# Re-spacing the memory projections, moving the zeroing and the first loads to other engines, and merging the memory update into the attention stage

## The chip, the cores and the metric

The kernel runs on one core of one Trainium2 chip. The metric is device time in microseconds (us), lower is better. Most executions of one kernel agree within a few tenths of a per cent. The engines are called as in the profile: PE is TensorE (matmuls), DVE is VectorE, ACT is ScalarE, POOL is GpSimd, and SP is SyncE, which here only issues DMA transfers. "1.00" as granted clock means that PE ran at full speed.

## The reference

The output is the concatenation of two independent parts over 2048 tokens of width 1024:

```python
def _A_ref(...):                        # complex diagonal state-space scan
    for t in range(L):
        h = Lam_bar[None, :] * h + Bu[:, t, :]
    y = 2.0 * einsum(hseq, Cmat).real + x * Dskip

def _B_ref(x, mem0, Wq, Wk, Wv, Wo, seg_len):     # 64 segments of 32 tokens, 8 memory tokens, 32 heads x 128
    mem = mem0
    for s in range(n_seg):
        h = concatenate([mem, x[segment s]])       # 40 tokens
        q, k, v = h @ Wq, h @ Wk, h @ Wv
        p = softmax(mask(q @ k.T * scale))
        o = (p @ v) @ Wo
        mem = o[:, :M, :]                          # memory for the next segment
        outs.append(o[:, M:, :])
```

The recurrence over `mem` looks serial. The kernel guesses the memory of all segments, computes everything in parallel with the guess, computes the new memory, and sets a flag if it differs too much; only then would it go round again. The trace holds one pass.

## The kernel before

The kernel runs in stages, with times read from the trace of before: part A (0 to 336 us); phase 1a, the K and V projections of part B (PE's last one ends at 834 us); phase 1b (844.5 to 1147 us), the Q projections, the guess of the memory and the projections of that guess ("memory projections"); the attention stage (1147 to 1655 us), 32 units of 4 segments x 16 heads; and the memory update with its flag (to the end).

Phase 1b goes through eight blocks of 512 weight columns. Each memory projection needs three 1 MB weight tiles (Wq, Wk, Wv); the Wq tile can be shared with the Q projection of the same block. The guess is ready only after block 2, so blocks 3 to 5 do two memory projections each, the second one for an early block:

```python
    wp  = tile_pool(name="p2_w", bufs=5)        # weights of Q and memory projections
    sp1 = tile_pool(name="p2_stg1", bufs=1)     # staging of the memory projections' results
    ...
    LAG = 3
    early = list(range(LAG))
    for hb in range(HB):
        wq = q_x(hb)                            # 128 matmuls of 512 columns, stores qT
        ...                                     # three steps of the guess
        if hb >= LAG:
            memproj(hb, wq)                     # stores qmT, kmT, vm of this block
            if early:
                memproj(early.pop(0))
    for hb in early:
        memproj(hb)
```

The attention stage first zeroes its block-diagonal buffers, then loads two units ahead. The rows of V that belong to the memory ("vmx") come in 16 small transfers per unit, half issued by SP and half by ACT. ACT then copies the memory columns of K and Q into place, behind its own issues:

```python
        for t in qmp + vmx + PTx + PTm + PTxm + PTmm:
            Gp.memset(t[:], 0.0)                                   # L458, POOL
        def load(u):
            nc.sync.dma_start(d["qT"][:], ...)
            nc.scalar.dma_start(d["kT"][:], ...)
            nc.sync.dma_start(km_u, ...); nc.sync.dma_start(qm_u, ...)
            nc.scalar.dma_start(d["v"][:], ...)
            for j in range(J):
                for b in range(4):
                    ...
                    (nc.sync if (j * 4 + b) % 2 == 0 else nc.scalar).dma_start(dst, src)   # L482
            S.activation(d["kT"][:, :, :, 0:M], km_u[:], ACT.Copy)   # L484, the K copy
            S.activation(<diagonal of qmp>, qm_u, ACT.Copy)
        ...
        load(0); load(1); front(0)
        for u in range(NU):
            if u + 1 < NU:
                front(u + 1)        # scores (PE), softmax (DVE, POOL, ACT), transposes (DVE)
            back(u)                 # probabilities x V (PE)
            if u + 2 < NU:
                load(u + 2)
            ...                     # half an output projection
```

The order of this text is not the order on PE: the build reorders the instructions of each engine within their dependencies, and fixes that order.

The memory update stands after the attention stage, in pools of its own: for each of 8 blocks 32 matmuls (L401), then DVE's differences and squares, two sums by matmul, and at the end the flag.

## Time and profile before

| | before |
|---|---|
| median of 15 runs | 1691.72 us (1685.87 to 1694.79) |
| span of the profiled run | 1686.6 us |
| PE busy | 1460.4 us, 87% |
| mean granted clock | 0.946 |

The first view is the page of the profile of before, its busy table and two rows of its slices (each digit is the busy share, or the clock, of one fortieth of the span, in tenths):

```profile
PE 1460.4 (87%) x14297; PEld 762.0 (45%) x14297; DVE 819.9 (49%) x1851; ACT 425.5 (25%) x793; POOL 165.4 (10%) x257
...
PE   4888989889999999999799988892888788877776
...
PEclk9899999899999999999999999896899989999998
```

PE is the engine that bounds the kernel, and one slice stands out: the digit 2, around 1160 us, where the attention starts, with a clock digit of 6 to 8 around it.

The windows view shows phase 1b in five stretches. Its columns are: the stretch, its length and PE's busy time, then the busy time of the other engines, and at the end the granted clock, the mean busy share of the DMA engines (as it is counted, it can come out a little above 1), and GB/s.

```profile
844.50:966.00 121.50, 117.22 (x917) 58.17 (x918) 37.14 (x89) 21.74 (x38) 2.10 (x6) 0.98 0.51 159
966.00:1010.00 44.00, 38.29 (x282) 20.57 (x280) 10.98 (x18) 9.90 (x19) 0.00 (x0) 0.92 0.76 226
1010.00:1050.00 40.00, 34.74 (x256) 18.40 (x255) 11.10 (x18) 9.27 (x18) 0.00 (x0) 0.96 0.88 254
1050.00:1090.00 40.00, 33.81 (x237) 17.41 (x235) 9.89 (x17) 8.40 (x17) 0.00 (x0) 0.87 0.83 249
1090.00:1147.00 57.00, 57.00 (x366) 28.81 (x363) 15.82 (x25) 13.70 (x25) 0.00 (x0) 1.00 0.63 185
```

PE is idle for 17.2 us in the three middle stretches, where the doubled memory projections are (44.00 - 38.29, and so on), and not at all in the last. The stretches with idle time also have a lower clock. What PE waits for there is in the view of waits, PE in phase 1b (what waited, on what: us in total, times, longest):

```profile
PE s_p L633 <- DMA p_w<-in_B_Wv_dram: 9.4, 3, 5.0
PE p_p L679 <- DMA p_w<-in_B_Wq_dram: 4.4, 2, 3.5
PE s_p L624 <- ACT s_stvd L253: 2.0, 3, 0.7
PE p_p L679 <- DVE p_stq L255: 1.7, 2, 1.4
```

Weight loads and evacuations, then. The evacuations are late because DVE in turn waits until a store has emptied the single staging buffer (view of waits, DVE, 955 to 1145 us):

```profile
DVE s_st L255 <- DMA b_qmT_s<-s_st: 20.7, 3, 13.1
```

The start of the attention is in the timeline of ACT (start, duration, engine, line; "ACTq" is ACT issuing a transfer, "x4" four of them; in brackets the idle time before, and what ended it). For the same time the windows view gives one line:

```profile
1156.37 7.11 ACTq L482 DMA_DIRECT2D s_vmx<-b_vm_s  x4
1163.59 0.63 ACT L484 ACTIVATE s_kT<-s_km 128x512 bf16<-128x512 bf16 x1 [15.31 <-DMA s_vmx<-b_vm_s]
...
1167.94 5.79 ACTq L482 DMA_DIRECT2D s_vmx<-b_vm_s  x8
1173.77 0.63 ACT L484 ACTIVATE s_kT<-s_km 128x512 bf16<-128x512 bf16 x1 [9.03 <-DMA s_vmx<-b_vm_s]
```
```profile
1147.00:1181.80 34.80, 3.10 (x258) 2.99 (x257) 9.38 (x19) 5.98 (x13) 17.01 (x17) 0.55 0.78 243
```

In both units the K copy comes directly after a batch of vmx issues, and PE, which needs the K copy for its scores, is busy 3.1 of 34.8 us at about half the clock.

### The profile page before, as it was taken

How to read it: one execution, taken by the hardware profiler on the slowest of the kernel's cores; microseconds unless marked ns; L12 is line 12 of the kernel's file. 1: busy time of each engine (PE TensorE's matmuls, PEld its weight loads, DVE VectorE, ACT ScalarE, POOL GpSimd, SP SyncE). 2: the span in 40 equal slices, each digit the busy share in tenths (PEclk: the TensorE clock that was granted, in tenths of full speed). 3: DMA queues.
4: the chain of work that ended last, by engine and by line, in shares of the span. 5: the costliest groups of instructions: out<-in, count | busy, mean ns of one | idle time of the engine just before them, and what ended most of it. 6: DMA issues, size and time to landing. Idle time of an engine off the chain costs nothing.

```text
span 1686.6 us, 33729 instructions
## 1 busy us (share of the span) xinstructions
PE 1460.4 (87%) x14297; PEld 762.0 (45%) x14297; DVE 819.9 (49%) x1851; ACT 425.5 (25%) x793; POOL 165.4 (10%) x257
## 2 busy tenths in 40 slices
PE   4888989889999999999799988892888788877776
PEld 2443434444444444444345444441545444544444
DVE  8999999632121221121123322222656666566664
ACT  7742322111111111111121122221322232322322
POOL 1100000020000000000000000004222222222220
PEclk9899999899999999999999999896899989999998
DMA  2420000395334343441473488866444545444423
GB/s 88 138 82 19 26 19 13 101 318 188 113 110 155 113 159 106 149 152 51 151 234 117 125 243 262 246 186 211 132 153 138 158 137 160 157 143 153 138 93 108
DMA packets 223112, 233.72 MB, mean 139 GB/s; under 512 B 61152, under 2 KB 194016, under 8 KB 222952
## 3 DMA queue, kind: packets, MB, share of 16 engines
q1 hardware_dynamic: 152880, 130.13, 24.8%
q10 hardware_dynamic: 68024, 95.04, 17.2%
q0 software_dynamic: 2048, 6.30, 1.1%
q8 instruction: 114, 1.87, 0.5%
q14 instruction: 46, 0.38, 0.1%
HBM read 150.99 MB, written 80.45 MB: 137 GB/s over the span
## 4 chain that ended last, share of the span: by engine, by line
PE 55%; DVE 27%; DMA 7%; POOL 5%; ACT 3%; issue 2%; SPq 1%; POOLq 0%; ACTq 0%; DVEq 0%
PE p_p L309 13%; PE p_p L322 13%; PE p_p L679 12%; PE s_pY L577 6%; DVE s_PTx L535 4%; DVE a_wr L177 2%; DVE a_wi L178 2%; POOL s_Sxx L502 2%; PE s_pO L555 2%; PE s_pO L554 2%; POOL s_Pxx L509 2%; DVE s_Sxx L498 1%; DVE s_sumx L505 1%; DVE s_mxx L501 1%; ACT s_Sxx L503 1%
## 5 line engine op out<-in xcount | busy, mean ns | idle before, releaser
L577 PE MATMUL s_pY<-b_Wo,s_oT 128*128 128x512 bf16 x1024 | 250.4, 399 | 4.6 <-issue 2.7
L679 PE MATMUL p_p<-g_shared,p_w 128*128 128x512 bf16 x1024 | 230.6, 386 | 17.6 <-POOL s_PTmm L458 10.2
L309 PE MATMUL p_p<-g_shared,p_w 128*128 128x512 bf16 x1024 | 224.3, 381 | 3.4 <-DMA p_w<-in_B_Wk_dram 3.4
L322 PE MATMUL p_p<-p_w,g_shared 128*128 128x512 bf16 x1024 | 224.8, 379 | 0.0
L679 PEld LDWEIGHTS <-p_w 128*128 128x128 bf16 x1024 | 100.9, 99 | 144.5 <-issue 14.8
L577 PEld LDWEIGHTS <-s_oT 128*128 128x128 bf16 x1024 | 99.7, 102 | 127.4 <-issue 24.6
L309 PEld LDWEIGHTS <-p_w 128*128 128x128 bf16 x1024 | 100.0, 98 | 124.0 <-DMA p_w<-in_B_Wk_dram 3.5
L322 PEld LDWEIGHTS <-g_shared 128*128 128x128 bf16 x1024 | 98.4, 98 | 118.4 <-issue 3.0
L554 PE MATMUL s_pO<-s_PTx,s_v 128*128 128x128 bf16 x512 | 77.8, 235 | 81.5 <-DVE s_PTx L535 73.0
L255 DVE CAST p_stk<-p_p 128x512 bf16<-128x512 f32 x64 | 44.3, 692 | 192.2 <-PE p_p L309 185.9
L255 DVE CAST p_st<-p_p 128x512 bf16<-128x512 f32 x64 | 44.3, 692 | 181.5 <-PE p_p L322 181.5
L255 DVE CAST p_stq<-p_p 128x512 bf16<-128x512 f32 x64 | 44.2, 691 | 163.4 <-PE p_p L679 145.6
L535 DVE STREAM_TRANSPOSE s_PTx<-s_Pxx 32x512 bf16<-32x512 bf16 x128 | 89.9, 703 | 45.1 <-POOL s_Pxx L509 43.7
L554 PEld LDWEIGHTS <-s_v 128*128 128x128 bf16 x512 | 52.8, 105 | 89.6 <-issue 45.3
L253 ACT ACTIVATE p_st<-p_p 128x512 bf16<-128x512 f32 x64 | 38.2, 597 | 201.5 <-PE p_p L322 201.5
L253 ACT ACTIVATE p_stk<-p_p 128x512 bf16<-128x512 f32 x64 | 38.2, 597 | 179.6 <-PE p_p L309 168.0
L165 PEld LDWEIGHTS <-g_shared 128*128 128x128 bf16 x512 | 51.7, 102 | 70.3 <-issue 21.8
L253 ACT ACTIVATE p_stq<-p_p 128x512 bf16<-128x512 f32 x64 | 37.7, 597 | 168.9 <-PE p_p L679 134.9
L165 PE MATMUL a_ur<-a_xT,g_shared 128*128 128x512 bf16 x256 | 70.0, 411 | 9.1 <-DVE a_ta L173 9.1
L556 ACT ACTIVATE s_oT<-s_pO 128x512 bf16<-128x512 f32 x128 | 70.0, 593 | 25.6 <-PE s_pO L555 25.0
L458 POOL MEMSET s_qmp<- 128x2048 bf16 x3 | 5.4, 1805 | 721.2 <-DMA b_v_s<-p_st 484.3
L555 PE MATMUL s_pO<-s_PTm,s_vmx 128*128 128x128 bf16 x512 | 74.9, 236 | 0.6
(197 smaller groups left out, 1931.4 us busy)
## 6 DMA issues: line engine op xcount, KB each, us to landing
s_kT<-b_kTa_s ACTq DMA_DIRECT2D x34, 640.0 KB
b_kTa_s<-p_stk ACTq DMA_DIRECT2D x8, 2560.0 KB
p_w<-in_B_Wq_dram SPq DMA_DIRECT2D x19, 1024.0 KB
s_v<-b_v_s ACTq DMA_DIRECT2D x34, 512.0 KB
p_w<-in_B_Wk_dram ACTq DMA_DIRECT2D x16, 1024.0 KB
b_v_s<-p_st SPq DMA_DIRECT2D x8, 2048.0 KB
b_qT_s<-p_stq SPq DMA_DIRECT2D x16, 1024.0 KB
s_qT<-b_qT_s SPq DMA_DIRECT2D x32, 512.0 KB
```

The costliest lines, as they stand in the source:

```text
L165: PE.matmul(u[:], BT[i][:, kc, pc * 128:(pc + 1) * 128], xT[:, kc, :], start=(kc == 0), stop=(kc == KC - 1))
L177: V.tensor_tensor_scan(wr[:], rb, wr[:], 0.0 if ini is None else ini[:, 0:1], ALU.mult, ALU.add)
L253: self.nc.scalar.activation(out, in_, ACT.Copy)
L255: self.nc.vector.tensor_copy(out, in_)
L309: PE.matmul(p[:], w[1][:, c, h4 * 128:(h4 + 1) * 128], xT[:, c, tb * 512:(tb + 1) * 512], start=(c == 0), stop=(c == KC - 1))
L322: PE.matmul(p[:], xT[:, c, tt * 128:(tt + 1) * 128], w[2][:, c, :], start=(c == 0), stop=(c == KC - 1))
L535: V.transpose(ptx[q, j, :, :].rearrange("p h k -> p (h k)"), Px[q, :, :].rearrange("p h k -> p (h k)"))
L554: PE.matmul(pO[:, b, :], v_u[:, h * E:(h + 1) * E], ptx[:, :, h, :], start=True, stop=False)
L555: PE.matmul(pO[:, b, :], vx[:, h, :], ptm[:, :, a, :], start=False, stop=True)
L556: S.activation(oT[:, 4 * a:4 * a + 4, :], pO[:], ACT.Copy)
L577: PE.matmul(pY[:], st[2 * gi + h // HH]["oT"][:, h % HH, :], Wo_sb[:, h, half * 512:(half + 1) * 512], start=(h == 0), stop=(h == H - 1))
L679: PE.matmul(p[:], wq[:, c, h4 * 128:(h4 + 1) * 128], xT[:, c, tb * 512:(tb + 1) * 512], start=(c == 0), stop=(c == KC - 1))
```

## The change

It has four parts:

- **Memory projections.** Projections 0 to 7 are spread anew, starting right behind the guess in block 2 and ending in block 6, so that the last block is a pure Q projection. The weights of the memory projections get four buffers of their own, and the staging is doubled.
- **Zeroing.** The attention buffers are zeroed by DVE in place of POOL.
- **Queue.** For the first two units, ACT's half of the vmx loads is issued by POOL.
- **Memory update.** It is moved into the attention stage, in front of the last output projections, in buffers that the attention no longer needs.

The diff, cut to its core (a second, switched-off path in part A, which leaves part A as it was built before, and the body of the update are left out):

```diff
-    b_step2(tc, scr, res, out, list(range(G)), True, dedup=skip_step1)
+    b_step2(tc, scr, res, out, list(range(G)), True, dedup=skip_step1,
+            mid_hook=lambda ...: b_step3(...))        # the former code of the memory update
...
         for t in qmp + vmx + PTx + PTm + PTxm + PTmm:
-            Gp.memset(t[:], 0.0)
+            V.memset(t[:], 0.0)
...
-                    (nc.sync if (j * 4 + b) % 2 == 0 else nc.scalar).dma_start(dst, src)
+                    (nc.sync if (j * 4 + b) % 2 == 0 else nc.gpsimd if do_x and u < 2 else nc.scalar).dma_start(dst, src)
...
+            if u == NU - 1 and mid_hook is not None:
+                fin = mid_hook(...)                   # the update's matmuls
             if u % 2 == 1:
                 outproj(u // 2, 0)
...
+        if mid_hook is not None:
+            fin()                                     # the flag
         outproj(NU // 2 - 1, 1)
...
-        wp = ctx.enter_context(tc.tile_pool(name="p2_w", bufs=5))
+        wp = ctx.enter_context(tc.tile_pool(name="p2_w", bufs=3))
-        sp1 = ctx.enter_context(tc.tile_pool(name="p2_stg1", bufs=1))
+        sp1 = ctx.enter_context(tc.tile_pool(name="p2_stg1", bufs=2))
+                wm_box.append(ctx.enter_context(tc.tile_pool(name="p2_wm", bufs=4)))   # at the first memproj
...
-        LAG = 3
-        early = list(range(LAG))
+        plan = {2: [2], 3: [3, 0], 4: [4, 1], 5: [5], 6: [6, 7]}
```

More of the change, by code (lines that the diff above doesn't have):

```diff
@@ L20 @@
 HALF_PI = 1.5707963
+POOL_POST = False
 def make_ident(nc, pool, name="ident"):
@@ L194, in stage1 @@
             V.tensor_tensor(h[:, 0, :], n1[:], n2[:], ALU.subtract)
-            V.tensor_tensor(n1[:], gr[:], s6, ALU.mult)
-            V.tensor_tensor(n2[:], gi[:], c6, ALU.mult)
-            V.tensor_tensor(h[:, 1, :], n1[:], n2[:], ALU.add)
+            if POOL_POST:
+                n3 = wp.tile([128, TB], BF16, name="a_n3"); n4 = wp.tile([128, TB], BF16, name="a_n4")
+                G.tensor_tensor(n3[:], gr[:], s6, ALU.mult)
+                G.tensor_tensor(n4[:], gi[:], c6, ALU.mult)
+                V.tensor_tensor(h[:, 1, :], n3[:], n4[:], ALU.add)
+            else:
+                V.tensor_tensor(n1[:], gr[:], s6, ALU.mult)
+                V.tensor_tensor(n2[:], gi[:], c6, ALU.mult)
+                V.tensor_tensor(h[:, 1, :], n1[:], n2[:], ALU.add)
             hblk[tb].append(h)
@@ L385, in b_body @@
                 b_memproj(tc, scr, res, w, hb, sp, ps, False, ev)
-    b_step2(tc, scr, res, out, list(range(G)), True, dedup=skip_step1)
-    NV = NT - M
-    with ExitStack() as ctx:
-        sp = ctx.enter_context(tc.tile_pool(name="s3_sb", bufs=2))
-        ps = ctx.enter_context(tc.tile_pool(name="s3_ps", bufs=2, space=PSUM))
-        pa = ctx.enter_context(tc.tile_pool(name="s3_pa", bufs=1, space=PSUM))
-        accd = pa.tile([1, NV], FP32, name="s3_accd"); accn = pa.tile([1, NV], FP32, name="s3_accn")
-        for dc in range(KC):
-            old = sp.tile([128, NV], FP32, name="s3_old")
-            nc.sync.dma_start(old[:], scr["m32"][:, dc, M:NT])
-            new = sp.tile([128, NV], FP32, name="s3_new")
-            if skip_step1:
-                ND = J * M + NSEG - J
-                p = ps.tile([128, ND], FP32, name="s3_p")
-                for h in range(H):
-                    PE.matmul(p[:], Wo_sb[:, h, dc * 128:(dc + 1) * 128], omT[:, h, 0:ND], start=(h == 0), stop=(h == H - 1))
-                S.activation(new[:, 0:J * M], p[:, 0:J * M], ACT.Copy)
-                S.activation(new[:, J * M:NV].rearrange("p (s i) -> p s i", i=M), p[:, J * M:ND - 1].unsqueeze(2).to_broadcast([128, NSEG - J - 1, M]), ACT.Copy)
-            else:
-                p = ps.tile([128, NT], FP32, name="s3_p")
-                for h in range(H):
-                    PE.matmul(p[:], Wo_sb[:, h, dc * 128:(dc + 1) * 128], omT[:, h, :], start=(h == 0), stop=(h == H - 1))
-                S.activation(new[:], p[:, 0:NV], ACT.Copy)
-            nc.sync.dma_start(scr["m32"][:, dc, M:NT], new[:])
-            V.tensor_tensor(old[:], new[:], old[:], ALU.subtract)
-            dsq = sp.tile([128, NV], BF16, name="s3_dsq"); nsq = sp.tile([128, NV], BF16, name="s3_nsq")
-            V.tensor_tensor(dsq[:], old[:], old[:], ALU.mult)
-            S.activation(nsq[:], new[:], ACT.Square)
-            PE.matmul(accd[:], cst["ones"][:], dsq[:], start=(dc == 0), stop=(dc == KC - 1))
-            PE.matmul(accn[:], cst["ones"][:], nsq[:], start=(dc == 0), stop=(dc == KC - 1))
-            V.tensor_copy(mT[:, dc, M:NT], new[:])
@@ new lines, in b_body, with b_step3, acc, fin @@
+    b_step2(tc, scr, res, out, list(range(G)), True, dedup=skip_step1,
+            mid_hook=lambda ps_tile, pa_tile, sb_tile: b_step3(tc, scr, res, tol, skip_step1, ps_tile, pa_tile, sb_tile))
+def b_step3(tc, scr, res, tol, dedup, ps_tile, pa_tile, sb_tile):
+    nc = tc.nc
+    V, Gp, S, PE = nc.vector, nc.gpsimd, nc.scalar, nc.tensor
+    mT = res["mT"]; Wo_sb = res["Wo"]; omT = res["omT"]; cst = res["cst"]
+    NV = NT - M
+    accd = pa_tile([1, NV]); accn = pa_tile([1, NV])
+    pend = []
+    olds = []
+    for i in range(KC // 2):
+        o2 = sb_tile((0, 0, 2, 2)[i], [128, 2, NV], FP32)
+        nc.sync.dma_start(o2[:], scr["m32"][:, 2 * i:2 * i + 2, M:NT])
+        olds.append(o2)
+    def acc(dc, dsq, nsq):
+        PE.matmul(accd[:], cst["ones"][:], dsq[:], start=(dc == 0), stop=(dc == KC - 1))
+        PE.matmul(accn[:], cst["ones"][:], nsq[:], start=(dc == 0), stop=(dc == KC - 1))
+    for dc in range(KC):
+        old = olds[dc // 2][:, dc % 2, :]
+        new = sb_tile(1, [128, NV], FP32)
+        if dedup:
+            ND = J * M + NSEG - J
+            p = ps_tile([128, ND])
+            for h in range(H):
+                PE.matmul(p[:], Wo_sb[:, h, dc * 128:(dc + 1) * 128], omT[:, h, 0:ND], start=(h == 0), stop=(h == H - 1))
+            S.activation(new[:, 0:J * M], p[:, 0:J * M], ACT.Copy)
+            S.activation(new[:, J * M:NV].rearrange("p (s i) -> p s i", i=M), p[:, J * M:ND - 1].unsqueeze(2).to_broadcast([128, NSEG - J - 1, M]), ACT.Copy)
+        else:
+            p = ps_tile([128, NT])
+            for h in range(H):
+                PE.matmul(p[:], Wo_sb[:, h, dc * 128:(dc + 1) * 128], omT[:, h, :], start=(h == 0), stop=(h == H - 1))
+            S.activation(new[:], p[:, 0:NV], ACT.Copy)
+        if pend:
+            acc(*pend.pop())
+        nc.sync.dma_start(scr["m32"][:, dc, M:NT], new[:])
+        V.tensor_tensor(old, new[:], old, ALU.subtract)
+        dsq = sb_tile(4, [128, NV], BF16); nsq = sb_tile(3, [128, NV], BF16)
+        V.tensor_tensor(dsq[:], old, old, ALU.mult)
+        S.activation(nsq[:], new[:], ACT.Square)
+        pend.append((dc, dsq, nsq))
+        V.tensor_copy(mT[:, dc, M:NT], new[:])
+    def fin():
+        acc(*pend.pop())
@@ L417, in b_body @@
         if "dbg" in res:
-            dbt = sp.tile([1, 2, NV], FP32, name="s3_dbg")
+            dbt = sb_tile(1, [1, 2, NV], FP32)
             V.tensor_copy(dbt[:, 0, :], accd[:]); V.tensor_copy(dbt[:, 1, :], accn[:])
             nc.sync.dma_start(res["dbg"], dbt[:])
-        thr = sp.tile([1, NV], FP32, name="s3_thr")
+        thr = sb_tile(0, [1, NV], FP32)
         V.tensor_scalar(thr[:], accn[:], tol * tol, None, ALU.mult)
         V.tensor_tensor(thr[:], accd[:], thr[:], ALU.is_gt)
-        fl = sp.tile([1, 1], FP32, name="s3_fl")
+        fl = sb_tile(4, [1, 1], FP32)
@@ L425, in b_body, with b_step2_gen @@
         V.tensor_reduce(fl[:], thr[:], AX.X, ALU.max)
         V.tensor_copy(res["flag"][:], fl[:])
+    return fin
 def diag_ap(t, dims):
     return bass.AP(t.tensor, t.offset, [list(t.ap[0])] + [list(d) for d in dims])
-def b_step2_gen(tc, scr, res, out, groups, do_x, nbuf=2, dedup=False):
+def b_step2_gen(tc, scr, res, out, groups, do_x, nbuf=2, dedup=False, mid_hook=None):
     nc = tc.nc
@@ L601, in b_step2_gen @@
                 load(u + 2)
+            if u == NU - 1 and mid_hook is not None:
+                tags = ("s2_qT", "s2_v", "s2_kT", "s2_km", "s2_qm")
+                fin = mid_hook(lambda shp: psS.tile(shp, FP32, name="s2_pS"), lambda shp: psO.tile(shp, FP32, name="s2_pO"),
+                               lambda i, shp, dt: ld.tile(shp, dt, name=tags[i]))
             if u % 2 == 1:
@@ L605, in b_step2_gen, with b_step2 @@
                 outproj(u // 2 - 1, 1)
+        if mid_hook is not None:
+            fin()
         outproj(NU // 2 - 1, 1)
-def b_step2(tc, scr, res, out, groups, do_x, dedup=False):
-    for _ in b_step2_gen(tc, scr, res, out, groups, do_x, dedup=dedup):
+def b_step2(tc, scr, res, out, groups, do_x, dedup=False, mid_hook=None):
+    for _ in b_step2_gen(tc, scr, res, out, groups, do_x, dedup=dedup, mid_hook=mid_hook):
         pass
@@ L708, in guess_gen @@
                 V.tensor_copy(res["mTd"][:, :, J * M:], res["mT"][:, :, J * M:NT].rearrange("p c (s i) -> p c s i", i=M)[:, :, :, 0])
+        wm_box = []
         def memproj(hb, wq=None):
+            if not wm_box:
+                wm_box.append(ctx.enter_context(tc.tile_pool(name="p2_wm", bufs=4)))
             w = [wq, None, None]
@@ L713, in memproj @@
                 if w[i] is None:
-                    w[i] = wp.tile([128, KC, 512], BF16, name="p2_w")
+                    w[i] = wm_box[0].tile([128, KC, 512], BF16, name="p2_wm")
                     (nc.scalar if i != 0 else nc.sync).dma_start(w[i][:], Wf[i][:, :, hb * 512:(hb + 1) * 512])
@@ L729, in b_phase1b @@
                         done = True
-            if hb >= LAG:
+            for m in plan.get(hb, []):
                 assert done
-                memproj(hb, wq)
-                if early:
-                    memproj(early.pop(0))
-        for hb in early:
-            memproj(hb)
+                memproj(m, wq if m == hb else None)
 def part_b(tc, x, mem0, Wq, Wk, Wv, Wo, out, ident, shared=None, n_static=1, dynamic=True, tol=2.0 ** -8, guess=True, dbg=None, xT_ready=False):
```

## The prediction

> **What bounds it now.** PE is busy 1460 of 1687 us (busy table), so only PE's idle time can be won. The windows view puts it in part A (0-336 us: 55 us idle, DVE full and untouched), in softmax waits of the attention stage (1182-1643, steady order unchanged), and in four places the change touches:
> - 834-844.5: 10.2 us before the first Q projection, waiting for a weight load issued only at 838.7 (timeline).
> - 966-1090: doubled memory projections. Timeline: PE waits 5.0, 2.4, 2.0 us for Wv, 0.8 and 3.5 for Wq, the rest for evacuations: 17 us, at a granted clock of 0.87-0.96. DVE waits 20.7 us for the single staging buffers (waits view).
> - 1147-1182: PE busy 3.3 of 35 us. The last projection's stores run to about 1154; POOL memsets take 13.3 us; 32 small vmx loads share two queues and block ACT's K copies (waits 15.3 and 9.0 us).
> - 1655-1687: memory update after the last attention unit, about 19 us for 14.7 us of matmuls, then 3.5 us of DVE after PE's end, then 9 us to the end.
>
> **Costing the change.**
> 1. Memory projections moved from blocks 3-7 to 2-6, separate weight buffers (3+4 for 5), double staging. Staging waits vanish. But a double projection still needs five tiles from four buffers, so the last Wv still waits for a release; a loaded 1 MB load took 11-13 us, and PE has about 8 us of work to cover it. New: projection 2 follows the guess directly. Its operand was ready 7.6 us after the guess's last matmul, with 3.3 us of matmuls now between; its Wk/Wv loads wait for the guess's memory and DMA stores (one waited 5.1 us). I charge 6 us. Net gain 7 us.
> 2. Transition: last is now the Q projection with one 1 MB store instead of 2.5 MB. Zeroing on DVE: the 128x2048 uint32 memset took 1.77 us, so estimated 6.5 us for all, against 13.3 on POOL, and off the load path. (The Trainium skill, "VectorE: DVE Perf Modes", "Zero memsets can be issued as uint32", gives the halving; the trace agrees.) Half the first vmx loads go to POOL, 0.54 us issue each (part A), 8.6 us, ending as its first softmax work arrives. ACT is freed, but Exp of unit 0 now stands behind a K copy of unit 2, and unit 2's scores stand before unit 0's output matmuls on PE. Estimate: 28 us from the last projection to the first output matmul against 34.7, with unit 2's scores already done: gain 8 us.
> 3. Memory update inside the attention: 48 of its 256 matmuls fill the last unit's wait, but push 11 projection matmuls later; flag arithmetic hides under the last output projection. DVE's 8 x 1.78 us still paces it, and a new output store comes last. Gain 4 us.
>
> **Predicted: 1671 us** (-1.2%), 80% range 1653 to 1685. Faster by over 2%: 0.20; within 2%: 0.79; slower: 0.01.
>
> **Right or wrong in the profile:** busy PE time unchanged within 10 us; stall of 4-8 us at the first b_mTd matmul; staging waits gone, one Wv wait left per double projection; last projection to first PTx matmul 25-31 us; no PE work after the last output projection; attention pace 14.9 us per unit unchanged.
>
> **What would make it wrong:** loads no longer colliding, so that phase 1b runs without stalls and at full clock (gain 15-20 more); POOL or SP queues delaying vmx so that the transition gains nothing; the tail's end being set by the last store.

## The result, and the profile after

Ratios here and below are the mean time of one kernel's fast runs over that of the kernel before, from the same rounds on the same chip, so they are not quite the ratio of the medians that are quoted. Intervals are 95%.

| | before | after |
|---|---|---|
| median | 1691.72 us (15 runs) | 1665.31 us (8 runs, 1661.09 to 1668.03) |
| ratio | | 0.9845 [0.9831, 0.9859] |
| span of the profiled run | 1686.6 us | 1657.9 us |
| mean granted clock | 0.946 | 0.956 |

The change gains 26.4 us, 1.6%; the profiled run of after is at the fast end of its runs, so the two traces differ by 28.7 us. To see where that came from, cut both traces at events that exist in both: the first Q projection matmul, PE's end of phase 1b, the first matmul of probabilities with V (unit 0's output matmul, "PTx matmul"), DVE's 5th, 29th and 30th copy of an output half, and the end. Each number is the length of one section in us, from the timelines, and good to 0.1 us or so.

| section | before | after | difference |
|---|---|---|---|
| start to first Q projection | 844.5 | 843.1 | -1.4 |
| phase 1b | 302.5 | 290.3 | -12.2 |
| transition: end of 1b to first PTx matmul | 34.7 | 35.5 | +0.8 |
| ramp: to the 5th output copy | 84.5 | 74.0 | -10.5 |
| steady attention: to the 29th output copy | 361.5 | 358.6 | -2.9 |
| 29th to 30th output copy | 4.9 | 4.8 | -0.1 |
| tail: to the end | 53.8 | 51.6 | -2.2 |

Two sections hold most of it, phase 1b and the ramp. The transition, for which the prediction had counted 8 us, did not get shorter.

The page of after:

```profile
PE 1448.9 (87%) x14297; PEld 758.6 (46%) x14297; DVE 828.1 (50%) x1869; ACT 426.2 (26%) x793; POOL 156.5 (9%) x255
...
PE   4799989889999999999979899994888787877777
...
PEclk9999999999999999999989999997899999999998
```

The same number of matmuls took 11.5 us less of busy time. The windows of phase 1b in after show where a part of it comes from:

```profile
843.10:966.00 122.90, 116.28 (x955) 59.81 (x956) 38.33 (x92) 23.45 (x42) 2.10 (x6) 0.95 0.50 158
966.00:1010.00 44.00, 43.41 (x304) 22.64 (x303) 13.00 (x21) 10.99 (x21) 0.00 (x0) 1.00 1.07 319
1010.00:1050.00 40.00, 36.15 (x263) 19.08 (x262) 10.93 (x18) 10.16 (x19) 0.00 (x0) 0.96 0.98 294
1050.00:1090.00 40.00, 40.00 (x251) 20.04 (x250) 10.36 (x16) 8.53 (x15) 0.00 (x0) 1.00 0.75 226
1090.00:1134.00 44.00, 41.23 (x282) 21.38 (x280) 12.74 (x21) 11.24 (x21) 0.00 (x0) 1.00 0.52 144
```

Summed over the five stretches, PE was busy 281.1 us of 302.5 before and 277.1 of 290.9 after. So its idle time in phase 1b fell from 21.4 to 13.8 us (7.6 us), and its busy time by another 4.0 us, for the same matmuls, because the clock was granted fully in two stretches more (in the first stretch it was a little lower, 0.95 against 0.98). By the clock records of the traces, PE was at half clock for 26.1 us of phase 1b before and for 15.1 us after. The Trainium skill, "TensorE: Matmul & The Clock Gate", "Part 1: The HAM clock gate", says that PE falls to half its clock after some 3.4 us of idleness and gets it back only after as long a busy time. Within phase 1b the half clock comes for 3.41, 6.83 or 10.24 us at a time, and it came with PE's wait of 5.0 us before and with those of 4.3 and 3.85 us after. But two shorter waits of before brought it too. Windows of before laid on two half-clock stretches, and the two waits that came just ahead of them in the timeline of PE:

```profile
1030.77 3.35 PE L633 MATMUL s_p<-p_w,b_mTd 128*92 128x512 bf16 x8 [2.39 <-DMA p_w<-in_B_Wv_dram]
...
1074.17 2.39 PE L633 MATMUL s_p<-p_w,b_mTd 128*92 128x512 bf16 x8 [1.97 <-DMA p_w<-in_B_Wv_dram]
```
```profile
1031.05:1034.46 3.41, 3.08 (x8) 1.10 (x6) 0.00 (x0) 0.00 (x0) 0.00 (x0) 0.50 1.09 380
1075.42:1085.66 10.24, 6.70 (x17) 2.20 (x16) 1.64 (x3) 1.14 (x2) 0.00 (x0) 0.50 1.02 301
```

So a wait of 2.39 us and one of 1.97 us were each followed by half clock within 1.3 us (the 3.5 us wait for Wq came only later, at 1076.56), while after's wait of 2.20 us was not. In these traces a wait of 2 us or more may cost twice, as idle time and as clock.

What is left of the waits in phase 1b, PE, after:

```profile
PE s_p L664 <- DMA p_wm<-in_B_Wv_dram: 6.6, 3, 3.8
PE s_p L655 <- DVE b_mTd L739: 4.3, 1, 4.3
```

All waits for Wq and for evacuations within the memory projections are gone, and the one for the guess's result (`b_mTd`) is new. DVE's waits for staging stores have left its list altogether.

The start of the attention, in the timelines of ACT and PE and in the windows view:

```profile
1147.69 0.63 ACT L509 ACTIVATE s_kT<-s_km 128x512 bf16<-128x512 bf16 x1 [15.36 <-DMA s_km<-b_kmT_s]
...
1153.60 0.63 ACT L509 ACTIVATE s_kT<-s_km 128x512 bf16<-128x512 bf16 x1 [2.93 <-DMA s_km<-b_kmT_s]
...
1159.91 0.74 ACT L528 ACTIVATE s_Sxx<-s_Sxx 128x640 f32<-128x640 f32 x1 [0.77 <-DMA s_vmx<-b_vm_s]
```
```profile
1148.38 0.72 PE L548 MATMUL s_pS<-s_kT,s_qT 128*32 128x40 bf16 x64 [14.95 <-ACT s_kT L509]
...
1154.99 0.72 PE L548 MATMUL s_pS<-s_kT,s_qT 128*32 128x40 bf16 x64 [3.41 <-ACT s_Sxm L521]
...
1165.59 0.72 PE L548 MATMUL s_pS<-s_kT,s_qT 128*32 128x40 bf16 x64 [9.21 <-DMA s_qT<-b_qT_s]
```
```profile
1133.40:1168.90 35.50, 4.58 (x394) 4.32 (x393) 18.88 (x45) 7.20 (x15) 14.10 (x25) 0.57 0.78 249
```

The two K copies now lie 6 us apart, not 10. PE still waits 15 us for the first, because the km load landed only then. It then waits 9.2 us for unit 2's qT, whose load SP issued at 1159.99, behind its own sixteen vmx issues. The transition is as long as before. Unit 0's softmax shows why (timelines of DVE and POOL):

```profile
1154.97 0.32 DVE L526 TENSOR_REDUCE s_mxm<-s_Sxm 128x4 f32<-128x160 f32 x1 [5.20 <-ACT s_Sxm L521]
1155.20 0.81 DVE L526 TENSOR_REDUCE s_mxx<-s_Sxx 128x16 f32<-128x640 f32 x1
```
```profile
1156.10 1.26 POOL L527 TENSOR_TENSOR s_Sxx<-s_Sxx,s_mxx 128x640 f32<-128x640 f32 x1 [0.62 <-DVE s_mxx L526]
```

Split at unit 0's steps, the transition is this (us):

| step | before | after |
|---|---|---|
| end of 1b to the first scores | 17.2 | 15.0 |
| first scores to the end of POOL's first subtraction | 3.7 | 9.0 |
| from there to ACT's Exp | 6.9 | 2.6 |
| Exp to unit 0's last transpose (s_PTm) | 7.0 | 6.8 |
| last transpose to the first PTx matmul | 0.0 | 2.2 |

The first scores come 2.2 us earlier and Exp waits 4.3 us less. But in the order that the build made for after, ACT waits 1.7 us for unit 0's qm load and 2.9 us for unit 1's km load before it evacuates unit 0's scores (s_Sxm); DVE's row maxima stand behind that evacuation, and 5.3 us are lost there. The last 2.2 us are eight score matmuls of unit 3, which stand in front of the first PTx matmul and wait for ACT.

PE has done 392 score matmuls in the transition (three units and a little of a fourth), where it had done 256 (two units) before. That shows in the ramp, where the output copies 1 to 4 come 14, 21, 25 and 28 us earlier than before (12.9 us of it because the first PTx matmul comes that much earlier).

At the end of after, PE's last matmuls are those of the last output projection (until 1648.4 us), and the flag is done at 1643.57, hidden. Before, the update's matmuls ended at 1672.4, their sums at 1675.7 and the flag came at 1677.37, alone.

### The profile page after: what moved, and what is told of

The parts are those of the page before. It is cut to its first block, busy times and chain, and to the rows that moved or that the text cites. A ratio compares the mean times of both kernels' runs of the same rounds, so it can differ in the third digit from the quotient of the medians.

```text
span 1657.9 us, 33748 instructions
## 1 busy us (share of the span) xinstructions
PE 1448.9 (87%) x14297; PEld 758.6 (46%) x14297; DVE 828.1 (50%) x1869; ACT 426.2 (26%) x793; POOL 156.5 (9%) x255
## 4 chain that ended last, share of the span: by engine, by line
PE 56%; DVE 26%; DMA 9%; POOL 4%; ACT 2%; issue 2%; SPq 1%; ACTq 0%; POOLq 0%
PE p_p L316 13%; PE p_p L329 13%; PE p_p L710 12%; PE s_pY L602 5%; DVE s_PTx L560 3%; DVE a_wi L179 2%; DVE a_wr L178 2%; DMA s_vmx<-b_vm_s 2%; POOL s_Sxx L527 2%; PE s_pO L580 2%; DMA p_wm<-in_B_Wv_dram 2%; PE s_pO L579 2%; DVE s_Sxx L523 1%; POOL s_Pxx L534 1%; DVE s_mxx L526 1%
## 5 line engine op out<-in xcount | busy, mean ns | idle before, releaser
L710 PE MATMUL p_p<-g_shared,p_w 128*128 128x512 bf16 x1024 | 229.4, 385 | 10.5 <-DMA p_w<-in_B_Wq_dram 10.5
L216 PE MATMUL a_py<-a_CT,a_h 128*128 128x512 bf16 x256 | 66.8, 385 | 9.9 <-DVE a_h L195 9.8
```

Source lines behind the costliest of these rows:

```text
L216: PE.matmul(py[:], hs[pc][:, 0, tt * 128:(tt + 1) * 128], CT[0][:, pc, half * 512:(half + 1) * 512], start=(pc == 0), stop=False)
L710: PE.matmul(p[:], wq[:, c, h4 * 128:(h4 + 1) * 128], xT[:, c, tb * 512:(tb + 1) * 512], start=(c == 0), stop=(c == KC - 1))
```

## The experiments

Twelve kernels ran, all with correct results, all timed against before in five rounds, in four sessions on four chips; between sessions the ratio to before is the safer comparison. Diffs are against the kernel named.

| kernel | base | median us | ratio | phase 1b | score matmuls before first PTx | transition | ramp | tail |
|---|---|---|---|---|---|---|---|---|
| before | | 1691.7 | 1 | 302.5 | 256 | 34.7 | 84.5 | 53.8 |
| after | | 1665.3 | 0.9845 [0.9831, 0.9859] | 290.3 | 392 | 35.5 | 74.0 | 51.6 |
| only_proj | before | 1679.9 | 0.9929 [0.9903, 0.9955] | 290.6 | 256 | 35.3 | 85.3 | 54.2 |
| zero_queue | before | 1688.7 | 0.9978 [0.9951, 1.0004] | 300.9 | 256 | 35.7 | 85.5 | 56.6 |
| only_update | before | 1685.9 | 0.9954 [0.9924, 0.9983] | 305.8 | 256 | 35.6 | 86.2 | 49.8 |
| undo_queue | after | 1676.1 | 0.9900 [0.9873, 0.9927] | 291.2 | 256 | 34.6 | 84.7 | 49.3 |
| undo_zero | after | 1673.4 | 0.9891 [0.9874, 0.9908] | 293.0 | 416 | 41.1 | 72.9 | 51.8 |
| undo_pair | after | 1673.5 | 0.9905 [0.9875, 0.9934] | 290.9 | 256 | 35.3 | 85.2 | 51.5 |
| pool_for_sp | after | 1675.1 | 0.9895 [0.9880, 0.9911] | 293.0 | 256 | 35.0 | 85.4 | 50.4 |
| pool_all | after | 1676.9 | 0.9924 [0.9901, 0.9947] | 293.1 | 416 | 43.8 | 73.7 | 53.6 |
| stg1 | after | 1669.8 | 0.9870 [0.9849, 0.9891] | 297.3 | 392 | 35.8 | 73.8 | 49.7 |
| wm5w2 | after | 1659.9 | 0.9802 [0.9783, 0.9820] | 283.9 | 392 | 36.2 | 75.0 | 51.7 |
| km_first | after | 1668.3 | 0.9864 [0.9844, 0.9885] | 290.5 | 416 | 35.3 | 74.8 | 50.4 |
| late2 | after | 1668.5 | 0.9856 [0.9835, 0.9878] | 293.8 | 392 | 35.4 | 74.1 | 49.9 |

The last five columns come from one profiled run of each kernel, cut at the events named above. One profiled run can be some 5 us off its kernel's median (its steady section alone varied from 358.6 to 367.6 us), so the columns are read for what repeats across kernels.

The count of score matmuls ahead of the first PTx matmul is not something that happens at run time: it is the order on PE that the build fixed. Compared matmul by matmul over the first ten output copies, six of the seven kernels with 256 have one and the same order on PE (all but zero_queue), and after, stg1, wm5w2 and late2 share another, up to 20 missing records of some 2400. Changing the issuing engine of a load changed the order on PE, ACT and DVE as well as the time of the load, and no run here parts the two.

### The parts one by one (only_proj, zero_queue, only_update, undo_queue)

The theory was that the parts are separate and that the start of the attention is gained by the zeroing and the queue. The rival was that the new plan of the memory projections mends both, because the last stores are out of the way earlier.

**only_proj**: before, with the new plan, weight buffers and staging alone.

```diff
+        plan = {2: [2], 3: [3, 0], 4: [4, 1], 5: [5], 6: [6, 7]}
+        # p2_w: 3 buffers, p2_wm: 4, p2_stg1: 2; nothing else of the change
```

> The kernel before with the memory projections' new plan and pools alone. Theory A (the parts are separate): phase 1b shortens by 12 us as in the profile of after, and the attention starts as slowly as before (first output copy about 13 us less well placed than in after): time about 1679 us, ratio 0.993. Rival B (the late burst of memory stores and loads made the attention's start slow, so the new plan alone mends both): about 1667 us, ratio 0.985.

Measured: 1679.9 us, ratio 0.9929, 12 us gained by the medians. Phase 1b is as short as in after, the ramp is that of before. The rival's 1667 us is excluded: the plan alone does not mend the attention's start.

**zero_queue**: before, with zeroing and queue alone.

```diff
-            Gp.memset(t[:], 0.0)
+            V.memset(t[:], 0.0)
-                    (nc.sync if (j * 4 + b) % 2 == 0 else nc.scalar).dma_start(dst, src)
+                    (nc.sync if (j * 4 + b) % 2 == 0 else nc.gpsimd if do_x and u < 2 else nc.scalar).dma_start(dst, src)
```

> The kernel before with zeroing on DVE and half of the first two units' vmx loads on POOL, nothing else. Theory A: it gains the 13 us of the attention's start alone, about 1679 us, ratio 0.992. Rival B: under 4 us, ratio 0.998 or more.

Measured: 1688.7 us, ratio 0.9978, with an interval that includes 1. With the old plan the pair is worth some 4 us by the ratio and at most some 8 us by its interval, not the 13 us that the first theory wanted. In its trace, ramp and transition are those of before. ACT no longer issues vmx loads there, but SP issued seven of unit 0's in 10.3 us from 1154.05 on, and unit 1's km load stood behind them (1164.76), so unit 1's K copy came at 1170.2. In after, both units' qT and km loads were issued by 1142.0, ahead of SP's vmx loads. So ACT free of issues is not enough: here the order on PE is still the one with two units ahead.

**only_update**: before, with the memory update merged into the attention.

```diff
-    b_step2(tc, scr, res, out, list(range(G)), True, dedup=skip_step1)
-    ...                                      # the update, in pools of its own
+    b_step2(..., mid_hook=lambda ...: b_step3(...))
```

> The kernel before with the memory update moved into the attention stage, nothing else. Both theories: the tail shortens by 2 to 3 us, nothing before 1600 us moves: about 1689 us, ratio 0.998 to 0.999. If the ratio is below 0.997 the tail is worth more than the profile of after shows.

Measured: 1685.9 us, ratio 0.9954, which is 6 to 8 us. Its tail is 49.8 us against 53.8. The rest of the gain is in no section of its profiled run, which was at the slow end of its runs (span 1690.2 us, clock 0.943). The interval, 3 to 13 us, includes the 4 us of the tail, so that there is a rest at all is not shown.

**undo_queue**: after, with ACT issuing its half of the first vmx loads again.

```diff
-                    (nc.sync if (j * 4 + b) % 2 == 0 else nc.gpsimd if do_x and u < 2 else nc.scalar).dma_start(dst, src)
+                    (nc.sync if (j * 4 + b) % 2 == 0 else nc.scalar).dma_start(dst, src)
```

> The kernel after with the first vmx loads back on SP and ACT. Theory A in its stronger form (ACT freed of vmx issues is what speeds the start): loses 10 us or more against after, ratio to before 0.991 or more. If zeroing on DVE or the new plan carries the start, it loses under 4 us: ratio 0.987 or less.

Measured: 1676.1 us, ratio 0.9900, so 9 to 11 us lost by one word in one line: what the theory wanted by the medians, a little short of its 0.991 by the ratio. The transition is as long as in after; the whole loss is in the ramp, 84.7 us against 74.0. The timeline of ACT in undo_queue:

```profile
1149.36 0.63 ACT L509 ACTIVATE s_kT<-s_km 128x512 bf16<-128x512 bf16 x1 [15.40 <-DMA s_km<-b_kmT_s]
...
1151.84 9.88 ACTq L507 DMA_DIRECT2D s_vmx<-b_vm_s  x16
1161.76 0.63 ACT L509 ACTIVATE s_kT<-s_km 128x512 bf16<-128x512 bf16 x1 [9.74 <-DMA s_vmx<-b_vm_s]
```

The first K copy comes as in after, 14 us after the end of phase 1b. Then ACT issues sixteen transfers for 9.9 us and only after that makes the K copy of unit 1, 12.4 us after the first where it was 5.9. Of the 9.88 us, the issues themselves took 4.6; the rest are waits of an issue until an earlier transfer on the same semaphore had landed. PE has two units' scores behind it at the first PTx matmul, not three; its order says so.

### Which half of the pair, which engine (undo_zero, pool_for_sp, pool_all, undo_pair)

**undo_zero**: after, with the zeroing back on POOL, the queue change kept.

```diff
-            V.memset(t[:], 0.0)
+            Gp.memset(t[:], 0.0)
```

> The changed kernel with the zeroing of the attention buffers back on POOL, the queue change kept. Theory A (the start of the attention is gained because ACT no longer issues half of the first vmx loads; who zeroes matters little): 1664 to 1669 us, ratio 0.984 to 0.987. Rival B (the zeroing is a necessary half, because POOL must now first zero for 13 us and only then issue its half of the vmx loads): first PTx matmul some 10 us later than in the changed kernel, 1673 to 1678 us, ratio 0.989 to 0.992, as bad as the run with the queue undone.

Measured: 1673.4 us, ratio 0.9891. The theory that who zeroes matters little has fallen; the rival's numbers are met. The timeline of POOL in undo_zero:

```profile
1142.16 3.55 POOL L483 MEMSET s_qmp<- 128x2048 bf16 x2 [234.47 <-DMA b_qT_s<-p_stq]
...
1154.80 4.94 POOL L507 DMA_DIRECT2D s_vmx<-b_vm_s  x9
1160.34 2.68 POOL L507 DMA_DIRECT2D s_vmx<-b_vm_s  x5 [0.61 <-DMA s_vmx<-b_vm_s]
```

POOL zeroes for 12.7 us and only then issues; in after its first eight were issued from 1143.45 on. The first PTx matmul comes 41.1 us after phase 1b, 5.7 us later than in after. Here the ramp is short (416 score matmuls were done), but the transition gives it back. In after, each zeroing of the same 512 KB took DVE 0.91 us, as 128 x 1024 uint32, where POOL took some 1.8 us (3.55 for two). That agrees with the Trainium skill, "VectorE: DVE Perf Modes", "Zero memsets can be issued as uint32", which says that the wider element halves the time; as two engines are compared, it is agreement and not a test.

**pool_for_sp**: after, with POOL taking SP's half in place of ACT's.

```diff
-  (nc.sync if (j * 4 + b) % 2 == 0 else nc.gpsimd if do_x and u < 2 else nc.scalar)
+  ((nc.gpsimd if do_x and u < 2 else nc.sync) if (j * 4 + b) % 2 == 0 else nc.scalar)
```

> The changed kernel with POOL taking SP's half of the first vmx loads and ACT keeping its own. Theory A (it is ACT that had to be relieved): no gain over the run with the queue undone, 1673 to 1678 us, ratio 0.989 to 0.992, output copies o2 to o4 as late as there. Rival C (any third queue will do, or SP is the better one to relieve, because unit 2's qT load stood behind SP's sixteen issues and PE waited 9.2 us for it): 1660 to 1667 us, ratio 0.981 to 0.986.

Measured: 1675.1 us, ratio 0.9895, the same as undo_queue. A third queue as such gives nothing: of the two reliefs, only that of ACT went with the gain. As the order on PE is that of undo_queue, ACT's time and the order are not told apart by it. Timeline of ACT in pool_for_sp, where the K copy again comes straight after its issues:

```profile
1155.27 7.61 ACTq L507 DMA_DIRECT2D s_vmx<-b_vm_s  x16
1162.92 0.63 ACT L509 ACTIVATE s_kT<-s_km 128x512 bf16<-128x512 bf16 x1 [9.75 <-DMA s_vmx<-b_vm_s]
```

This sharpens a sentence of the Trainium skill, "DMA: Bandwidth & Descriptors", "Issuing engines are not separate DMA queues": issuing from several engines "will only save the time on the sequencer it takes to initiate the DMA, which is usually small relative to the DMA itself". These runs agree for a single transfer, whose issue took ACT about 0.3 us where it took over 3 us to land. But sixteen of them came to 4.6 to 4.8 us of issuing, and with the waits between them to 7.6 to 9.9 us in front of a copy that PE waited for.

**pool_all**: after, with all 32 first vmx loads on POOL.

```diff
-  (nc.sync if (j * 4 + b) % 2 == 0 else nc.gpsimd if do_x and u < 2 else nc.scalar)
+  (nc.gpsimd if do_x and u < 2 else nc.sync if (j * 4 + b) % 2 == 0 else nc.scalar)
```

> The changed kernel with all 32 of the first two units' vmx loads on POOL, none on SP or ACT. In the changed kernel SP issued its sixteen in 8.8 us, unit 2's qT load behind them, and PE waited 9.2 us for it. Theory A (an engine that issues loads delays its own compute by 0.55 us each): POOL now issues for some 17.6 us from about 1143.5, so its first subtraction, at 1156.1 in the changed kernel, comes after 1161, and 4 to 8 us are lost: 1669 to 1674 us, ratio 0.987 to 0.990. Rival (POOL has slack there, and SP's late qT is what the attention's start waits for): unit 2's scores come 5 us or more earlier and 2 to 5 us are gained, 1660 to 1663 us.

Measured: 1676.9 us, ratio 0.9924, worse than the theory's range by 3 us and far from the rival's. Timeline of POOL in pool_all:

```profile
1170.47 0.54 POOL L507 DMA_DIRECT2D s_vmx<-b_vm_s  x1 [0.79 <-DMA s_vmx<-b_vm_s]
1171.03 1.27 POOL L527 TENSOR_TENSOR s_Sxx<-s_Sxx,s_mxx 128x640 f32<-128x640 f32 x1
```

POOL's first softmax subtraction started at 1171.0 us; in after it started at 1156.1. The 32 issues took longer than the 17.6 us that were estimated, because between them POOL also waited, 6.9 us in all, for earlier ones on the same semaphores to land (the program gives POOL eight semaphores in turn). Unit 2's scores did come 5.7 us earlier after the end of phase 1b than in after, as the rival said, and nothing was gained by it. So POOL is the right engine only for as many issues as fit ahead of its own first work.

**undo_pair**: after, with both halves undone.

```diff
-            V.memset(t[:], 0.0)
+            Gp.memset(t[:], 0.0)
-                    (... nc.gpsimd if do_x and u < 2 else nc.scalar).dma_start(dst, src)
+                    (... nc.scalar).dma_start(dst, src)
```

> The changed kernel with both halves of the change at the start of the attention undone: zeroing back on POOL and the first vmx loads back on ACT. Each half undone alone cost 8 to 9 us (ratios 0.9900 and 0.9891 against 0.9845). PE's order is that of the run with the queue undone. If the two halves are worth something only together (each alone gives nothing): 1673 to 1677 us, ratio 0.989 to 0.991, equal to either run with one half undone. Rival (they add up, each worth 8 to 9 us): 1681 to 1685 us, ratio 0.994 to 0.996. Third reading (the parts are additive over the whole change, so the product of the ratios of the runs with the projections alone and the update alone, 0.9929 x 0.9954 = 0.988, is what remains): 1670 to 1673 us, and then one half alone would do harm.

Measured: 1673.5 us, ratio 0.9905 [0.9875, 0.9934], equal to either half undone alone. That the halves add up (0.994 to 0.996) is excluded; the third reading (0.988) lies inside the interval and is not. So in these runs zeroing by DVE and issuing by POOL act as one change: the pair is worth 8 us (by the medians) to 10 us (by the ratios) with the new plan, and half of it nothing that these runs can see.

### Inside phase 1b (stg1, late2, wm5w2)

**stg1**: after, with single staging.

```diff
-        sp1 = ctx.enter_context(tc.tile_pool(name="p2_stg1", bufs=2))
+        sp1 = ctx.enter_context(tc.tile_pool(name="p2_stg1", bufs=1))
```

> The changed kernel with a single staging buffer for the memory projections, as before. Theory A (the doubled staging is a real part of the gain of phase 1b: before, DVE waited up to 20.7 us for a store to release it): 3 to 6 us of the 12 us are lost, 1668 to 1671 us, ratio 0.986 to 0.988. Rival B (the new plan spreads the projections so that the stores have time, and the second buffer is idle insurance): within 1.5 us of the changed kernel, 1664 to 1667 us. Against both: over 8 us lost.

Measured: 1669.8 us, ratio 0.9870, 4.5 us lost by the medians, within the theory's range; phase 1b is 6.9 us longer in its trace. The waits for the staging stores are back, in the view of waits of stg1, on DVE and ACT:

```profile
DVE s_st L262 <- DMA b_qmT_s<-s_st: 5.8, 1, 5.8
```
```profile
ACT s_st L260 <- DMA b_qmT_s<-s_st: 24.9, 2, 12.8
```

**late2**: after, with memory projection 2 after block 3.

```diff
-        plan = {2: [2], 3: [3, 0], 4: [4, 1], 5: [5], 6: [6, 7]}
+        plan = {3: [3, 2], 4: [4, 0], 5: [5, 1], 6: [6, 7]}
```

> The changed kernel with memory projection 2 after Q block 3 and not right behind the guess: blocks 3, 4, 5 and 6 then have two each. The prediction charged 6 us for the stall at the first use of the guess's result; the trace shows 4.27 us. If the stall is lost time that more Q work would cover: it goes (under 0.5 us left), but one more double projection brings one more Wv wait of 2 to 4 us, net gain 0 to 3 us, 1662 to 1666 us, ratio 0.982 to 0.985. Rival (the early projection 2 is what lets the later loads start early, DMA share 1.07 in that window): the waits of the later double projections grow, 1667 to 1672 us, ratio 0.985 to 0.988.

Measured: 1668.5 us, ratio 0.9856, within the rival's ranges, though the interval [0.9835, 0.9878] reaches into the other's. The trace decides for the rival: the stall of 4.3 us at the guess's result is gone, but the waits for Wv have grown from 6.6 to 12.9 us, and phase 1b is 3.5 us longer. View of waits, PE, late2:

```profile
PE s_p L664 <- DMA p_wm<-in_B_Wv_dram: 12.9, 4, 5.5
```

**wm5w2**: after, with the buffers divided five to two.

```diff
-        wp = ctx.enter_context(tc.tile_pool(name="p2_w", bufs=3))
+        wp = ctx.enter_context(tc.tile_pool(name="p2_w", bufs=2))
-                wm_box.append(ctx.enter_context(tc.tile_pool(name="p2_wm", bufs=4)))
+                wm_box.append(ctx.enter_context(tc.tile_pool(name="p2_wm", bufs=5)))
```

> The changed kernel with five buffers for the weights of the memory projections and two for those of the Q projections (the sum is kept, there is no room for more). The prediction said that five tiles from four buffers leave one wait for Wv in each double projection; the trace shows 0.6, 3.9 and 2.2 us of it. If the fifth buffer is what these lack: the three waits go and 4 to 6 us are gained, 1659 to 1662 us, ratio 0.981 to 0.983. Rival (a wait is only moved: with two buffers the Q projections wait for their weights instead, and the order of PE's work changes): 1664 us or more, and new waits for p_w on PE.

Measured: 1659.9 us, ratio 0.9802 [0.9783, 0.9820], the fastest kernel of the study; its interval lies below that of after, and below that of every other kernel here (against the line of 2% it is unclear, as the interval includes 0.98). It beats after by 5.4 us by the medians, by 7 us by the ratios. The waits for Wv are gone, at the price of one wait of 2.1 us for a Wq tile of a memory projection (view of waits, PE, wm5w2):

```profile
PE s_p L655 <- DVE b_mTd L739: 4.3, 1, 4.3
PE s_p L655 <- DMA p_wm<-in_B_Wq_dram: 2.1, 1, 2.1
```

Phase 1b is 283.9 us, 6.4 us shorter than in after. The rival was right in that the order of PE's work changed, and wrong in that this cost time. So the prediction's diagnosis, five tiles from four buffers, is shown by taking it away.

### The first load of the attention (km_first)

**km_first**: after, with km and qm loaded ahead of qT.

```diff
+            nc.sync.dma_start(km_u, ...); nc.sync.dma_start(qm_u, ...)
             nc.sync.dma_start(d["qT"][:], ...)
             nc.scalar.dma_start(d["kT"][:], ...)
-            nc.sync.dma_start(km_u, ...); nc.sync.dma_start(qm_u, ...)
```

> The changed kernel with the small km and qm loads of each unit issued ahead of the qT load on SP's queue. In the changed kernel the first scores wait 14.95 us for ACT's copy of km, and km landed 8 us after its issue, behind 1 MB transfers. Theory (km is late because it stands behind qT): the first scores 2 to 3 us earlier, and as much gained, 1662 to 1664 us, ratio 0.982 to 0.984. Rival (km is late because all the first loads share the DMA engines, 0.74 busy there, or qT itself is then the late one): first scores within 1 us of the changed kernel's 15 us after the last projection, 1664 to 1667 us.

Measured: 1668.3 us, ratio 0.9864, no gain. The K copy did come 2.2 us earlier (1145.49 against 1147.69), but the first scores came 14.6 us after the last projection, against 15.0 in after. Timeline of PE in km_first:

```profile
1147.90 0.73 PE L548 MATMUL s_pS<-s_kT,s_qT 128*32 128x40 bf16 x64 [14.57 <-DVE s_PTmm L483]
```

The view names DVE's zeroing, which ended at 1147.1, but that is the view's guess and not the cause: in after, PE's sequencer had passed its wait for DVE at 1145.4, while DVE zeroed until 1147.2. The semaphore updates in the trace of km_first tell what came last: qT, issued at 1140.18 behind km and qm, landed at 1147.50, and PE's sequencer passed its next wait at 1147.59. In after, with qT in front, qT had landed at 1144.80 and km at 1147.67. So the rival is met, in its second form: of km and qT, the one that is issued second is the late one. (The loads that stood ahead of km in after were of 512 and 640 KB, not of 1 MB.) In both kernels the first loads are issued within 0.2 us of the landing of the last qT store, 5.9 us after the end of phase 1b; what shortening that would give was not tried.

The run also settles another point. Here SP issued unit 2's qT load ahead of its vmx loads, and unit 2's scores came 26.2 us after the end of phase 1b, against 32.2 in after. The transition is still 35.3 us: PE's wait of 9.2 us for that load was not what made the transition long.

## Why the prediction was right or wrong

The prediction said 1671 us, range 1653 to 1685, with "within 2%" the likeliest outcome. Measured were 1665.3 us and a ratio of 0.9845. Total and direction were right; the terms behind it were not all right, and that the total came within 6 us is in part luck: 8 us that were counted did not come, and 10.5 us came in a stage for which next to no gain had been counted.

- **Phase 1b, 7 us predicted, 12.2 us in the trace.** The mechanism was right on every point that was named: stall at the guess's result 4.27 us (said 4 to 8; charged at 6), staging waits gone, one wait for Wv in each of the three double projections (0.6, 3.9 and 2.2 us). The idle time fell by 7.6 us, which is the predicted term. What was missing is the 4.0 us that the same matmuls took less because the clock recovered; the prediction had it only under what would make it wrong, at 15 to 20 us more, together with all stalls. only_proj shows the whole term alone: 12 us.
- **Transition, 8 us predicted, none found.** This is the step that failed: "28 us from the last projection to the first output matmul against 34.7, with unit 2's scores already done". The runs show 35.5 us. What was expected of a freed ACT and earlier stores did come, 2.2 us at the first scores and 4.3 us at Exp. What the prediction did not have is that ACT, in the new order, waits for unit 0's qm load and unit 1's km load before it evacuates unit 0's scores, which cost 5.3 us at the row maxima, and that eight scores of unit 3 stand before the first PTx matmul, which cost 2.2 us. The wait for a K copy that it did have, unit 2's in front of Exp, is in the 2.6 us that remain there. PE's long wait for unit 2's qT, behind SP's sixteen vmx issues, ran beside all this and did not set the length: km_first shortened it and the transition stayed.
- **In place of it came the ramp, 10.5 us.** In the seven traces with 256 score matmuls ahead of the first PTx matmul the ramp took 84.5 to 86.2 us (mean 85.3). In the seven with 392 or 416 it took 72.9 to 75.0 us (mean 74.0). No trace lies between, over four different ways of issuing the first vmx loads and two of zeroing; but these are few orders on PE, not fourteen (see above). The second half of the failed sentence, "with unit 2's scores already done", thus goes with the true gain, which is paid out one stage later, in units 0 to 4, and kept: the steady pace is 14.93 us per unit before and 14.90 after (9th to 29th output copy), as predicted. That the lead causes the short ramp is what these traces agree on; no kernel set the order on PE by itself with the loads as they were, so it is not shown apart from the loads, nor from the orders on ACT and DVE that go with it. This is the rival that stays open.
- **The lead is not enough.** undo_zero and pool_all have it and lose 6 to 8 us in the transition, because POOL is late: its first subtraction starts as soon as its last issue is done (1164.83 and 1171.03). A reading that fits all runs, but that is not shown part by part, is that the gain needs ACT free of the issues, POOL free to issue early, and the memory projections stored early, which the new plan gives; each of zero_queue, undo_queue, undo_zero and pool_for_sp lacks one of these.
- **Tail, 4 us predicted.** The pair of traces shows 2.2 us. The three kernels with the old update have tails of 53.8, 54.2 and 56.6 us, the eleven with the new one 49.3 to 53.6 us (mean 50.9), 4.0 us apart in the mean. No PE work is left after the last output projection, as said.
- **Busy PE "unchanged within 10 us"**: wrong, narrowly: 1460.4 to 1448.9 us. The granted clock rose from 0.946 to 0.956, and 4.0 of the 11.5 us are in phase 1b.

The means over all traces add up to nearly the measured gain. Phase 1b takes 303.1 us in the three traces with the old plan, and 291.6 in the eight with the new plan and its own buffers, staging and order; that is 11.5 us. Ramp 11.2, tail 4.0 and transition 0 make 26.7 us, against 26.4 us between the medians; with single traces that differ by some 5 us, so close an agreement is chance.

Open are: whether the order on PE or the freed ACT makes the short ramp, whether only_update gains more than its tail, and what the first 15 us of the attention would be if its first loads did not wait for the last qT store.

## What to carry to other kernels

A transfer that a compute engine issues is work in that engine's queue: ask what stands behind it, and give it to an engine that has nothing to do until after it, and only as many as fit in that time. When a stage starts late, look not only at when its first result comes but at how many units are in flight by then; a lead there can be kept through a steady stage that itself becomes no faster. When one wait is taken away and nothing moves, look for a second one that ends at nearly the same time, check in the trace which of them ended last before you believe the name that the view gives, and ask whether the build has changed the order on the engines. Where PE waits for several us at a time, count the clock as well as the idle time.

## What the Trainium skill lacked or had wrong

- "DMA: Bandwidth & Descriptors", "Issuing engines are not separate DMA queues": calls the issue time usually small. For one transfer that holds here (about 0.3 us on ACT against over 3 us to landing), but loads split into 16 small transfers kept ACT's sequencer for 9.88 us (undo_queue) and 7.61 us (pool_for_sp) in front of a 0.63 us copy that PE needed. 4.6 and 4.8 us of this were issuing.
- The same section does not say that an issue can itself have to wait: in pool_all, POOL's 32 issues of 0.54 us each came with 6.9 us of waits between them, for the earlier transfer on the same of this program's semaphores, so that its first arithmetic started 14.9 us later than in after (11.9 us, if the 3.1 us by which its phase 1b ended later are taken off).
- "TensorE: Matmul & The Clock Gate", "Part 1: The HAM clock gate", puts the fall to half clock after at least one idle window of about 3.4 us. In before it followed waits of 2.39 and 1.97 us (half clock from 1031.05 and 1075.42); in after, a wait of 2.20 us brought none. The 4.0 us of busy time that phase 1b lost without any change to its matmuls is a size for the clock's effect within a stage that PE keeps busy for over 90%.
- "VectorE: DVE Perf Modes": agrees (0.91 us on DVE against 1.8 us on POOL for 512 KB of zeros). That moving the zeroing also frees another engine's queue is a matter of this kernel: with the zeroing back on POOL, undo_zero lost 5.7 us in the transition.
